# One transformer block on one core: AV sums in column groups and turned by DMA, tokens of a tile ordered by parity, more LN1 turned by DMA, a modulation loaded in pieces, up evicted to bf16 by ScalarE, and a new order

## The chip, the core and the metric

The kernel runs on one NeuronCore of a Trainium2 chip. The core has five engines that take their instructions in order and wait for each other by semaphores: TensorE (PE, matmuls; its weight loads are shown apart as PEld), VectorE (DVE), ScalarE (ACT), GpSimd (POOL) and SyncE (SP), which here only issues DMAs. The metric is the device time of the kernel in microseconds. Three runs of the kernel before took 248.26, 248.86 and 251.65 us; the median is 248.86.

## The reference

S = 2048 tokens, D = 512, 32 heads of 16, a feed-forward width F = 1792, all bf16. Cut to what matters:

```python
mod = (silu(c) @ w_mod).reshape(1, 6, 1, -1)
sa, ca, ga, sb, cb, gb = ...            # six vectors of 512
h = layernorm(x) * (1 + ca) + sa
x = x + ga * A(h, wqkv, wo)
h = layernorm(x) * (1 + cb) + sb
x = x + gb * B(h, w1, w3, w2)

def A(x, wqkv, wo):                     # sliding local attention, W = 8, dilation 2
    q, k, v = heads(x @ wqkv)
    idx = pos[:, None] - 2 * arange(8)  # each token sees itself and 7 tokens of its own parity before it
    logits = einsum('bhsd,bhswd->bhsw', q, k[idx]) * 16 ** -0.5, masked where idx < 0
    o = einsum('bhsw,bhswd->bhsd', softmax(logits), v[idx])
    return o.reshape(B, S, D) @ wo

def B(x, w1, w3, w2):
    return (silu(x @ w1) * (x @ w3)) @ w2
```

## The kernel before

**How a program is made.** `_build` records operations, each with an engine, a function that emits its instructions, a cost and the values that it reads and writes. `Program.place` then sets them in the order of a literal list, `ORDER`, and gives each pooled buffer the slot that the literal list `SLOTS` names; `synchronize` adds the semaphore waits that follow from data and from buffer reuse. Each engine gets its share of `ORDER` and runs it strictly in order, SP's DMA issues included. So an instruction that waits holds back everything behind it on its engine. Nearly all DMAs are issued on SP, in L124, and one on ACT.

**Tiles.** The tokens are 16 tiles of 128. LN1 works on the groups of `LN1`, two tiles twice and then four tiles three times. The feed-forward part works on the groups of `FFN`: two, two, four, four, two and two tiles. Attention works on the `BLOCKS`, pairs of tiles.

**Start.** 26 matmuls on a constant (`warm`, L472) run while x and weights load. `modulation(0)` (L457) multiplies silu(c) with the first 1024 columns of w_mod, 32 matmuls of one column each, and writes shift and scale of LN1 to `modc`. `modulation(1)` does the same for LN2; `gate` (L485, L495) makes the two gates, with which wo (L876) and w2 (L882) are scaled.

**LN1 and projections.** `ln_stats` takes mean and variance on DVE (L509, L510) and the power on POOL, and writes the normalized rows `xn` (L521). `ln_T` turns them, features on partitions: with PE transposes (L581), whose eviction on ACT applies scale and shift (L589), or, for groups numbered from `DMA_T` on, with a DMA transpose on SP followed by one ACT pass (L566). `DMA_T = (5, 2)`: none of LN1, and LN2 from its third group on. `proj_qk` (L634) makes q and k, features on partitions, evicted on ACT (L642, L643); `proj_v` (L653) makes v, tokens on partitions, evicted (L663) and stored to a scratch tensor in DRAM.

**Attention of a tile.** DVE multiplies q with the eight shifted k (L684, 4096 elements per partition). PE sums over a head with 16 matmuls of 256 columns (L694): the weights are a 0/1 matrix `E` of 32 columns, and each matmul writes one of four groups of 32 output partitions, one group for 32 consecutive tokens. The softmax works in PSUM (L706, L711 on DVE, exp L724 on ACT, L736 to L739 on DVE). Its result `attn` is turned by PE (L749) and evicted (L753), so that partitions hold 16 tokens x 8 window places. Four DMAs per tile gather the shifted v from the scratch tensor in that layout (`vsh`, four times 256 KB), DVE multiplies (L769), and PE sums over the window:

```python
for g in range(8):
    for ft in range(KT):
        ins = e.matmul(b[:, ft * P + 16 * g:ft * P + 16 * g + 16], vv.at[:, g, ft * P:(ft + 1) * P], ind[:],
                       start=True, stop=True)
```

Here (L778) vsh is the stationary side and the 0/1 matrix `ind` of 16 columns moves, so the output already has features on partitions. ACT evicts it (L788), reordering tokens, and PE multiplies with wo (L795); DVE adds the residual and keeps its row sum (L799).

**Feed-forward.** Each of the 14 units of a group is four matmuls with w1 and four with w3 (L811), a silu on ACT (L817), and a product on DVE that reads `up` from PSUM (L820). w2 (L849, and L837 for the last two tiles) sums the 14 units; DVE adds the residual (L859), and SP stores the output. FFN units of early groups stand among the attention of later tiles in `ORDER`.

Of the kernel before, what the change touches and what calls it, by code (L numbers as in the profile page):

```python
# [248 lines left out]
C_PQ, C_RED, C_ACC = 2203, 455, 800  # L249
# [17 lines left out]
NWARM = 18  # L267
DMA_T = (5, 2)
# [3 lines left out]
def _build(p, A_x, A_wqkv, A_wo, B_w1, B_w3, B_w2, c, w_mod, out):  # L272
# [4 lines left out]
    x_view = x2d.rearrange("(t p) d -> p t d", p=P)  # L277
# [18 lines left out]
    atb = [sb([P, 2, 32, W], bf, f"attn{i}") for i in range(NSM)]  # L296
# [3 lines left out]
    otb = [sb([P, KT, P], bf, f"ot{i}") for i in range(2)]  # L300
# [3 lines left out]
    E_sb = sb([P, KT, H], bf, "E")  # L304
    ones = sb([P, 512], bf, "ones")
    ind = sb([P, 16], bf, "ind")
    before = sb([P, W, 2, 16], bf, "before")
# [8 lines left out]
    csT_bf = sb([P, KT], bf, "csT_bf")  # L316
    gcol = sb([P, 8], bf, "gcol")
    modc = sb([P, 16], f32, "modc")

# [32 lines left out]
    otpool = Pool("ot", otb)  # L352
    hhpool = Pool("hh", [])
    tmppool = Pool("tmp", [])

    def held(pool, items):

        vals = []
        for i, item in enumerate(items):
# [12 lines left out]
                                           pattern=[[-1, P]], channel_multiplier=1), 300, k, w=[vident])  # L372
    p.op("pool", lambda e: e.memset(cst[:, 0:1], EPS), 80, k, part=[vcst])
# [3 lines left out]
    p.op("pool", lambda e: e.affine_select(out=E_sb[:], in_=E_sb[:], compare_op=ALU.is_ge, fill=0.0, base=0,  # L377
                                           pattern=[[128, KT], [-16, H]], channel_multiplier=1), 320, k, w=[vE])
    p.op("pool", lambda e: e.affine_select(out=E_sb[:], in_=E_sb[:], compare_op=ALU.is_ge, fill=0.0, base=15,
                                           pattern=[[-128, KT], [16, H]], channel_multiplier=-1), 320, k, w=[vE])  # L380
    p.op("pool", lambda e: e.memset(ind[:], 1.0), 100, k, w=[vind])
    p.op("pool", lambda e: e.affine_select(out=ind[:], in_=ind[:], compare_op=ALU.is_ge, fill=0.0, base=0,
                                           pattern=[[-W, 16]], channel_multiplier=1), 200, k, w=[vind])
    p.op("pool", lambda e: e.affine_select(out=ind[:], in_=ind[:], compare_op=ALU.is_ge, fill=0.0, base=W - 1,
                                           pattern=[[W, 16]], channel_multiplier=-1), 200, k, w=[vind])
    p.op("pool", lambda e: e.memset(before[:], 0.0), 250, k, w=[vbefore])
    p.op("pool", lambda e: e.affine_select(out=before[:], in_=before[:], compare_op=ALU.is_ge, fill=BEFORE, base=0,
                                           pattern=[[-DIL, W], [1, 2], [2, 16]], channel_multiplier=0), 400, k, w=[vbefore])
# [10 lines left out]
    p.dma(x_sb[:, 0:2, :], x_view[:, 0:2, :], ("load", 1), (256, 1024), w=vx[0:2])  # L399
    p.dma(wm_s[0][:], wm_view[:, :, 0:1024], ("load", 2), (512, 2048), w=[vwms[0]])  # L400
    p.dma(x_sb[:, 2:4, :], x_view[:, 2:4, :], ("load", 27), (256, 1024), w=vx[2:4])
# [4 lines left out]
    for g in range(1, 4):  # L406
        p.dma(x_sb[:, 4 * g:4 * g + 4, :], x_view[:, 4 * g:4 * g + 4, :], ("load", 5 + g), (512, 1024), w=vx[4 * g:4 * g + 4])
# [35 lines left out]
    p.op("dve", lambda e: e.tensor_copy(csT_bf[:], bank(vpc).bitcast(bf)[:, 0:KT]), 180, ("mod", 1), r=[vpc], w=[vcs])  # L443
# [4 lines left out]
    def modulation(i):  # L448
        k = ("mod", 2 + i)
        vm = Val("ps_mod", psum)  # L450
        jlo = 8 * i

        def mm(e):
            b = bank(vm)
            for j in range(8):
                for t in range(KT):
                    ins = e.matmul(b[:, j:j + 1], wm_s[i][:, t, j * P:(j + 1) * P], csT_bf[:, t:t + 1], start=(t == 0),  # L457
                                   stop=(t == KT - 1))
            return ins

        o = p.op("pe", mm, 32 * 26, k, r=[vwms[i], vcs] + wm_hold, w=[vm])
        p.op("dve", lambda e: e.tensor_copy(modc[:, jlo:jlo + 4], bank(vm)[:, 0:4]), 180, k, r=[vm], part=[vmod[i]])
        p.op("dve", lambda e: e.tensor_scalar(modc[:, jlo + 4:jlo + 8], bank(vm)[:, 4:8], 1.0, None, op0=ALU.add), 180, k,
             r=[vm], part=[vmod[i]])
        return o

    def warm(i, after=()):

        vw = Val("ps_warm", psum)

        def mm(e):
            return e.matmul(bank(vw), ones[:, 0:P], ones[:], start=True, stop=True)  # L472

        p.op("pe", mm, 428 if i < 10 else 232, ("warm", i), r=[vc], w=[vw], after=after)

    def gate(i):
# [4 lines left out]
        def mm(e):  # L481
            b = bank(vm)
            for j in range(4):
                for t in range(KT):
                    ins = e.matmul(b[:, j:j + 1], wm_g[i][:, t, j * P:(j + 1) * P], csT_bf[:, t:t + 1], start=(t == 0),  # L485
                                   stop=(t == KT - 1))
            return ins
# [132 lines left out]
    def proj_qk(gi, Ts, kind, vh):  # L620
# [6 lines left out]
        for ft in range(KT):  # L627
# [3 lines left out]
            def mm(e, ts, ft=ft, vp=vp):  # L631
                col = kind * D + ft * P
# [7 lines left out]
            def ev(e, ft=ft, vp=vp):  # L640
                if kind == 0:
                    return e.activation(dstv.at[:, ft, at0:at0 + n], bank(vp)[:, 0:n], ACT.Copy, scale=SCALE)  # L642
                return e.activation(kT[:, ft, PAD + 512 * cch + at0:PAD + 512 * cch + at0 + n], bank(vp)[:, 0:n], ACT.Copy)  # L643
# [3 lines left out]
    def proj_v(T, tt, vh):  # L647
# [19 lines left out]
        p.dma(v_dram[PAD + T * P:PAD + (T + 1) * P, :], lambda: vt.at[:], k, (128, 1024), r=[vt], w=[vd], cost=400, store=True)  # L667
# [5 lines left out]
    def logits(Ts):  # L673

        vl = Val("ps_l", psum)
        for i, T in enumerate(Ts):
# [10 lines left out]

            def red(e, i=i, T=T, vp=vp):
                c0 = vl.at * 512 + i * W * 32
                if T == 0:  # L690
                    e.matmul(PALL[0:32, c0:c0 + W * 32], ones[:, 0:32], before[:], start=True, stop=False, tile_position=(0, 0))
                for ft in range(KT):
                    for q in range(4):
                        ins = e.matmul(PALL[32 * q:32 * q + 32, c0:c0 + W * 32], E_sb[:, ft, :], bass.AP(vp.at, ft * P + 32 * q, [[W * KT * P, P], [KT * P, W], [1, 2], [2, 16]]),  # L694
                                       start=(ft == 0 and (T > 0 or q > 0)), stop=(ft == KT - 1), tile_position=(0, 32 * q))
# [35 lines left out]
    def softmax(Ts, vl, ve, vx_):  # L731
# [7 lines left out]
        p.op("dve", lambda e: e.tensor_tensor(ve.at[0][:, 0:n], bass.AP(PALL, bank(vl).offset, [[8 * 512, P], [W * 32, n], [1, 32], [32, W]]),  # L739
                                              bass.AP(ve.at[2], 0, [[64, P], [32, n], [1, 32], [0, W]]), ALU.mult),  # L740
             74 + 267 * n, k, r=[vr, vx_], w=[va], hold=[ve, vl], lead=o, lock=False)
        vt, val = Val("ps_at", psum), Val("al", alpool)

        def turn(e):
            b = bank(vt).bitcast(bf)
            for i in range(n):
                at = b[:, i * 256:(i + 1) * 256].rearrange("p (q y h) -> p q y h", q=4, y=2)
                for y in range(2):
                    ins = e.transpose(at[:, :, y, :], bass.AP(ve.at[0], i * W * 32 + y * 16 * W, [[2 * W * 32, P], [1, P]]), ident[:])  # L749
# [7 lines left out]
    def values(T, i, val):  # L757
# [3 lines left out]
        for q in range(4):  # L761
            p.dma(lambda q=q: vv.at[:, 2 * q:2 * q + 2, :],
                  bass.AP(v_dram, (PAD + T * P + 32 * q) * D, [[2 * D, 16], [-DIL * D, W], [1, 2 * D]]), ("vl", T), (128, 2048),
# [8 lines left out]
        vo = Val("ps_o", psum)  # L772

        def acc(e):
            b = bank(vo)
            for g in range(8):
                for ft in range(KT):
                    ins = e.matmul(b[:, ft * P + 16 * g:ft * P + 16 * g + 16], vv.at[:, g, ft * P:(ft + 1) * P], ind[:],  # L778
                                   start=True, stop=True)
            return ins  # L780

        p.op("pe", acc, C_ACC, ("ac", T), r=[vv, vind], w=[vo])
        vt = Val("ot", otpool)

        def ev(e):
            dst = bass.AP(vt.at, 0, [[KT * P, P], [32, 4 * KT], [1, 2], [2, 16]])
            src = bass.AP(PALL, bank(vo).offset, [[8 * 512, P], [32, 4 * KT], [16, 2], [1, 16]])
            return e.activation(dst, src, ACT.Copy)  # L788

        p.op("act", ev, c_act(512), ("ac", T), r=[vo], w=[vt])  # L790
# [13 lines left out]
    def ffn_unit(gi, n, fi, vh, after):  # L804
# [4 lines left out]
        def mm(e, vp, wt):  # L809
            for t in range(KT):  # L810
# [9 lines left out]
        p.op("dve", lambda e: e.tensor_tensor(vh_.at[:, 0:n], vt.at[:, 0:n], bank(vup)[:, 0:n], ALU.mult), c_dve(n), k,  # L820
             r=[vt, vup], w=[vh_])
# [35 lines left out]
    def store(T, c0, n, vz):  # L857
        vo = Val("o", opool)
        p.op("dve", lambda e: e.tensor_tensor(vo.at[:, 0:n], bank(vz)[:, 0:n], x_sb[:, T, c0:c0 + n], ALU.add),  # L859
             c_dve(n), ("zo", T), r=[vz, vx[T]], w=[vo])  # L860
        finals.append(p.dma(out2d[T * P:(T + 1) * P, c0:c0 + n], lambda: vo.at[:, 0:n], ("zo", T), (128, 2 * n), r=[vo], cost=400, store=True))

    for i in range(NWARM):
        warm(i)
    first = modulation(0)
    for i in range(8):
        warm(NWARM + i, [first])
# [12 lines left out]
    for g in range(NG):  # L880
        a, b = cuts[g], cuts[g + 1]
# [19 lines left out]
    p.late = list(late.values())  # L901
    p.gates = [d[T] for T in range(NT) for d in (prods, avs)]
    for o, n in zip(p.late, GATES):
        if n >= 0:
            o.deps[p.gates[n]] = True
# [98 lines left out]
```

## Time and profile before

| | |
|---|---|
| device time, median of three runs | 248.86 us (248.26 to 251.65) |
| span of the profiled execution | 248.5 us |
| PE / DVE / ACT / POOL busy | 239.7 / 180.1 / 138.3 / 23.9 us |
| DMA moved | 35.74 MB in 33711 packets, 52.0% of 16 engines' span on the SP queue |
| granted TensorE clock | 1.000 |
| AV sums, L778 | 512 matmuls, 0.78 to 0.96 us for the 32 of a tile |
| logit sums, L694 | 256 matmuls of 256 columns |
| products in the FFN, L820 | 84 on DVE, 39.3 us |

The profile is of one execution, whose span runs from the first to the last instruction; its time is not told apart from the span, which lies 0.36 us below the median of the runs. Matmuls are pipelined, so the mean duration of one matmul in a group is longer than the distance to the next; the chain of work in order of time gives the distance. The same holds, less, for DVE and ACT, where two instructions in a row overlap by some 0.1 us: one L663 eviction lasts 0.60 us, two in a row span 1.09. An issue's "landing" is the time from its issue on SP to its completion.

### The profile page before, as it was taken

To read this page: it belongs to the slowest core of one execution; us is meant where nothing else is said; L and a number is where in the kernel's file an instruction comes from. 1 tells how busy PE (TensorE), PEld (TensorE's weight loads), DVE (VectorE), ACT (ScalarE), POOL (GpSimd) and SP (SyncE) were. 2 spreads that over 40 slices of the span, in tenths; PEclk is the share of its full clock that TensorE was granted. 3 is DMA by queue.
4 is the path that set the end of the run, shared out by engine and by line. 5 is a ranking of instruction groups with operands and counts; after the bars stand their busy time and mean duration, and the time that the engine had idled before them with its cause. 6 is when DMAs were issued, how large, how long until landed. Compare 5 with 4: busy or idle time off the path is not lost.

```text
span 248.5 us, 5309 instructions
## 1 busy us (share of the span) xinstructions
PE 239.7 (96%) x2194; PEld 148.5 (60%) x2224; DVE 180.1 (72%) x273; ACT 138.3 (56%) x273; POOL 23.9 (10%) x66
## 2 busy tenths in 40 slices
PE   7999998799999999999999999999999999999995
PEld 2587454458964549776544464455455556687864
DVE  4488997799999999999988998873182432452542
ACT  2189684699455799447659775263557305442300
POOL 6130200010300200022031002000100100000000
PEclk9999999999999999999999999999999999999999
DMA  6989799999903607886354828916002002100001
GB/s 222 355 265 289 207 246 331 299 320 268 303 18 78 176 3 191 243 247 170 28 150 131 228 66 209 192 21 193 0 14 52 3 0 63 63 3 21 3 34 51
DMA packets 33711, 35.74 MB, mean 144 GB/s; under 512 B 8584, under 2 KB 24984, under 8 KB 33688
## 3 DMA queue, kind: packets, MB, share of 16 engines
q1 hardware_dynamic: 33680, 35.42, 52.0%
q8 instruction: 17, 0.28, 0.5%
q14 instruction: 6, 0.05, 0.1%
q10 hardware_dynamic: 8, 0.00, 0.0%
HBM read 29.62 MB, written 4.21 MB: 136 GB/s over the span
## 4 chain that ended last, share of the span: by engine, by line
PE 89%; DVE 3%; DMA 3%; issue 2%; SPq 1%; ACT 0%; DVEq 0%
PE pall L811 39%; PE pall L849 17%; PE pall L634 7%; PE pall L795 5%; PE pall L778 5%; PE pall L653 4%; PE pall L472 3%; PE pall L694 3%; DMA sb_vsh<-v_scratch_dram 3%; PE pall L837 2%; PE pall L581 2%; SPq L124 1%; DVE sb_pq L684 1%; PE pall L457 1%; PE pall L749 1%
## 5 line engine op out<-in xcount | busy, mean ns | idle before, releaser
L811 PE MATMUL pall<-sb_h,sb_w 128*128 128x256 bf16 (+1 forms) x664 | 102.4, 307 | 0.4
L811 PEld LDWEIGHTS pall<-sb_h,sb_w 128*128 128x128 bf16 x672 | 64.5, 98 | 33.0 <-issue 0.6
L820 DVE TENSOR_TENSOR sb_hh<-sb_sg,pall 128x256 bf16<-128x256 bf16 (+1 forms) x84 | 39.3, 503 | 32.3 <-PE pall L811 28.7
L817 ACT ACTIVATE sb_sg<-pall 128x256 bf16<-128x256 f32 (+1 forms) x84 | 35.2, 453 | 47.4 <-PE pall L811 39.7
L849 PE MATMUL pall<-sb_w,sb_hh 128*128 128x512 bf16 x187 | 43.6, 379 | 0.6 <-issue 0.2
L684 DVE TENSOR_TENSOR sb_pq<-sb_q,sb_kT 128x4096 bf16<-128x4096 bf16 x16 | 36.3, 2282 | 0.1
L634 PE MATMUL pall<-sb_h,sb_wqkv 128*128 128x512 bf16 (+1 forms) x154 | 31.1, 335 | 1.0 <-DMA sb_wm_s<-in_w_mod_dram 0.6
L849 PEld LDWEIGHTS pall<-sb_w,sb_hh 128*128 128x128 bf16 x196 | 18.9, 98 | 20.7 <-issue 0.2
L769 DVE TENSOR_TENSOR sb_vsh<-sb_vsh,sb_al 128x4096 bf16<-128x4096 bf16 x12 | 27.3, 2286 | 2.0 <-DMA sb_vsh<-v_scratch_dram 2.0
L788 ACT ACTIVATE sb_ot<-pall 128x512 bf16<-128x512 f32 x16 | 11.9, 745 | 19.6 <-PE pall L778 19.5
L634 PEld LDWEIGHTS pall<-sb_h,sb_wqkv 128*128 128x128 bf16 x160 | 14.8, 97 | 10.9 <-ACT sb_v L663 0.7
L859 DVE TENSOR_TENSOR sb_o<-pall,sb_x 128x512 bf16<-128x512 f32 (+1 forms) x18 | 11.3, 629 | 13.4 <-DMA out_dram<-sb_o 7.2
L589 ACT ACTIVATE sb_h<-pall,sb_modc 128x256 bf16<-128x256 bf16 (+1 forms) x26 | 15.3, 669 | 10.0 <-PE pall L581 9.9
L653 PE MATMUL pall<-sb_wqkv,sb_h 128*128 128x512 bf16 x62 | 16.0, 379 | 0.1
L531 POOL TENSOR_SCALAR sb_nm<-sb_sx 128x2 f32<-128x2 f32 x8 | 3.7, 466 | 124.0 <-DVE sb_x L799 124.0
L799 DVE SCALAR_TENSOR_TENSOR sb_x<-pall,sb_x 128x512 bf16<-128x512 f32 x16 | 10.6, 686 | 6.3 <-PE pall L795 6.3
L795 PE MATMUL pall<-sb_wo,sb_ot 128*128 128x512 bf16 x60 | 14.7, 379 | 0.2
L535 ACT ACTIVATE sb_xn<-sb_x,sb_nm 128x512 bf16<-128x512 bf16 x16 | 11.5, 720 | 5.0 <-POOL sb_nm L531 4.9
L546 ACT ACTIVATE sb_xn<-sb_x,sb_nb,sb_rs 128x512 bf16<-128x512 bf16 x16 | 12.4, 810 | 3.2 <-POOL sb_nb L544 3.2
L778 PEld LDWEIGHTS pall<-sb_ind,sb_vsh 128*128 128x128 bf16 x384 | 11.1, 96 | 3.5 <-ACT sb_ot L788 1.5
L778 PE MATMUL pall<-sb_ind,sb_vsh 128*128 128x16 bf16 x384 | 11.4, 169 | 1.2 <-DVE sb_vsh L769 1.1
L509 DVE BATCH_NORM_STATS2 sb_st<-sb_x 128x6 f32<-128x512 bf16 x16 | 10.8, 672 | 2.3 <-DMA sb_x<-in_A_x_dram 2.3
(79 smaller groups left out, 224.7 us busy)
## 6 DMA issues: line engine op xcount, KB each, us to landing
sb_vsh<-v_scratch_dram SPq DMA_DIRECT2D x48, 256.0 KB, 4.9
sb_vshx<-v_scratch_dram SPq DMA_DIRECT2D x16, 256.0 KB, 4.1
sb_w<-in_B_w_dram SPq DMA_DIRECT2D x6, 512.0 KB, 9.3
sb_w<-in_B_w_dram SPq DMA_DIRECT2D x6, 384.0 KB, 6.9
v_scratch_dram<-sb_v SPq DMA_DIRECT2D x16, 128.0 KB, 3.7
out_dram<-sb_o SPq DMA_DIRECT2D x14, 128.0 KB, 1.9
sb_wqkv<-in_A_wqkv_dram SPq DMA_DIRECT2D x3, 512.0 KB, 7.8
sb_x<-in_A_x_dram SPq DMA_DIRECT2D x3, 512.0 KB, 9.1
```

The costliest lines, as they stand in the source:

```text
L546: p.op("act", lambda e, vn=vn, T=T: e.activation(vn.at[:], x_sb[:, T, :], ACT.Identity, bias=nb[:, T, :], scale=rs[:, NT + T, :]), c_act(5 ...
L589: return e.activation(vh.at[:, ft, 0:n * P], b[:, j * 512:j * 512 + n * P], ACT.Identity, bias=modc[:, 8 * which + ft:8 * which + ft + 1], ...
L634: ins = e.matmul(bank(vp)[:, 0:n], wqkv[:, t, col:col + P], vh.at[:, t, 0:n], start=(t == ORDER[0]), stop=(t == ORDER[-1]))
L653: ins = e.matmul(bank(vp), vh.at[:, t, tt * P:(tt + 1) * P], wqkv[:, t, 2 * D:3 * D], start=(t == ORDER[0]), stop=(t == ORDER[-1]))
L684: return e.tensor_tensor(vp.at[:], in0, in1, ALU.mult)
L769: return e.tensor_tensor(v_w, v_w, a_w, ALU.mult)
L778: ins = e.matmul(b[:, ft * P + 16 * g:ft * P + 16 * g + 16], vv.at[:, g, ft * P:(ft + 1) * P], ind[:], start=True, stop=True)
L795: ins = e.matmul(bank(vy), vt.at[:, ft, :], wo[:, ft, :], start=(ft == 0), stop=(ft == KT - 1))
L811: ins = e.matmul(bank(vp)[:, 0:n], wt[:, t, fi * P:(fi + 1) * P], vh.at[:, t, 0:n], start=(t == 0), stop=(t == KT - 1))
L817: p.op("act", lambda e: e.activation(vt.at[:, 0:n], bank(vgp)[:, 0:n], ACT.Silu), c_act(n), k, r=[vgp], w=[vt], table="silu")
L820: p.op("dve", lambda e: e.tensor_tensor(vh_.at[:, 0:n], vt.at[:, 0:n], bank(vup)[:, 0:n], ALU.mult), c_dve(n), k, r=[vt, vup], w=[vh_])
L849: ins = e.matmul(bank(vz), vhh[fi].at[:, tt * P:(tt + 1) * P], w2[:, fi, :], start=(fi == 0), stop=(fi == NF - 1))
```

## The change

The knobs: `DMA_T = (3, 2)` has LN1's tiles 8 to 15 turned by eight DMA transposes on SP. `NWARM` and `NWARM2` are 14 and 3, in all 17 matmuls where 26 were. `AVCOL` (all tiles) picks the new AV sum, `UPACT` (groups 0 to 3 of `FFN`, 56 units) the new eviction of up; `GBLATE` is off, so w2 is scaled as before. `GATES`, all -1 before, had no effect and is gone.

**Parity.** The 128 tokens of a tile stand on partitions with the 64 even ones first. Loads of x, stores of v and of the output are written so: x of tiles 0 and 1 in a DMA each, x of the others in DMAs of 64 partitions each. q and k keep the natural order in their buffers: their evictions write every other element. The features of q and k are interleaved, so that one `E` of 32 columns serves all four feature tiles; the weights for that are read with a step of four elements.

**AV.** With 32 tokens of one parity and four window places on the partitions of each gathered piece, the sum takes eight matmuls of 512 columns with the 0/1 matrix as the stationary side, 32 columns, in four column groups. The result has tokens on partitions; ACT evicts it contiguously (`oa`), and a DMA transpose on SP turns it into `ot`, which wo reads. The number and size of the gathers are the same. The last softmax product is two instructions of half the size.

**Modulation 0.** Its 1 MB of weights comes in four DMAs, one for each 128 rows, and the matmuls run piece by piece; the moving side, a slice of `csz`, has eight columns that are zero but for one, so that all products add up in the same eight output columns. One matmul more sets the base (0 or 1), and one copy replaces two DVE instructions.

**Up.** In the 56 units ACT copies up from PSUM to bf16 in SBUF, and DVE multiplies two bf16 tiles in SBUF.

**Order.** `ORDER` and `SLOTS` are new throughout. SP has 172 entries of DMA where 140 were: eight more loads, and 24 more transposes. On SP, the first eight gathers of v now stand ahead of all FFN weights, and behind four of the LN1 transposes; the q third of wqkv is the eleventh DMA, after 2 MB of x and w_mod. On PE, the first FFN unit stands behind all but two entries of the q and k projections, all but two of v, the logit sums of eight tiles and the AV sums of four.

```diff
-NWARM = 18
-DMA_T = (5, 2)
+NWARM = 14
+NWARM2 = 3
+DMA_T = (3, 2)
+AVCOL = frozenset(range(16))
+UPACT = frozenset((g, f) for g in range(4) for f in range(NF))
+GBLATE = False
...
-    p.dma(x_sb[:, 0:2, :], x_view[:, 0:2, :], ("load", 1), (256, 1024), w=vx[0:2])
-    p.dma(wm_s[0][:], wm_view[:, :, 0:1024], ("load", 2), (512, 2048), w=[vwms[0]])
...
+    def split_rows(a, row):
+        return bass.AP(a.tensor, a.offset + row * D, [[D, 2], [2 * D, P // 2], [1, D]])
+    def x_rows(T, n, r):
+        return bass.AP(x2d.tensor, x2d.offset + (T * P + r) * D, [[2 * D, P // 2], [P * D, n], [1, D]])
+    for T in range(2):
+        p.dma(x_sb[:, T, :], split_rows(x2d, T * P), ("load", 1), (128, 1024), w=[vx[T]])
+    for t in range(KT):
+        p.dma(wm_s[0][:, t, :], wm_view[:, t, 0:1024], ("load", 2), (128, 2048), w=[vwm0[t]])
+    for r in range(2):
+        p.dma(x_sb[64 * r:64 * r + 64, 2:4, :], x_rows(2, 2, r), ("load", 27), (128, 1024), part=vx[2:4])
...
+            if ts[0] == 0:
+                e.matmul(b[:, 0:8], ident[:], mbase[:], start=True, stop=False)
+            for t in ts:
+                for j in range(8):
+                    ins = e.matmul(b[:, 0:8], wm_s[i][:, t, j * P:(j + 1) * P], csz[:, t, 7 - j:15 - j], start=False,
+                                   stop=(t == KT - 1 and j == 7))
...
-                    ins = e.matmul(bank(vp)[:, 0:n], wqkv[:, t, col:col + P], vh.at[:, t, 0:n], start=(t == ORDER[0]),
+                    w_qk = bass.AP(wqkv, t * 3 * D + kind * D + ft, [[KT * 3 * D, P], [KT, P]])
+                    ins = e.matmul(bank(vp)[:, 0:n], w_qk, vh.at[:, t, 0:n], start=(t == ORDER[0]),
...
+                src = bank(vp)[:, 0:n].rearrange("p (t r m) -> p t r m", r=2, m=P // 2)
+                return e.activation(dst.rearrange("p (t m r) -> p t r m", r=2, m=P // 2), src, ACT.Copy,
+                                    scale=SCALE if kind == 0 else 1.0)
...
-        p.op("dve", lambda e: e.tensor_tensor(ve.at[0][:, 0:n], ..., ALU.mult),
+        for y in range(2):
+            o = p.op("dve", lambda e, y=y: e.tensor_tensor(bass.AP(ve.at[0], 128 * y, [[2 * W * 32, P], [W * 32, n], [1, 4], [4, 32]]),
...
-                    ins = e.matmul(b[:, ft * P + 16 * g:ft * P + 16 * g + 16], vv.at[:, g, ft * P:(ft + 1) * P], ind[:],
-                                   start=True, stop=True)
...
+                for y in range(2):
+                    for q in range(4):
+                        ins = e.matmul(b[32 * q:32 * q + 32, :], ind[:], vv.at[:, 4 * (q % 2) + 2 * y + q // 2, :], start=(y == 0),
+                                       stop=(y == 1), tile_position=(0, 32 * q))
...
+            p.op("act", lambda e: e.activation(va.at[:], bank(vo), ACT.Copy), c_act(512), ("ac", T), r=[vo], w=[va])
+            p.dma(lambda: vt.at[:], lambda: va.at[:], ("ac", T), (128, 1024), r=[va], w=[vt], cost=1250, transpose=True)
...
-        p.op("dve", lambda e: e.tensor_tensor(vh_.at[:, 0:n], vt.at[:, 0:n], bank(vup)[:, 0:n], ALU.mult), c_dve(n), k,
-             r=[vt, vup], w=[vh_])
+        if (gi, fi) in UPACT:
+            p.op("act", lambda e: e.activation(vh_.at[:, 0:n], bank(vup)[:, 0:n], ACT.Copy), c_act(n), k, r=[vup], w=[vh_])
+            p.op("dve", lambda e: e.tensor_tensor(vh_.at[:, 0:n], vt.at[:, 0:n], vh_.at[:, 0:n], ALU.mult), 60 + n * 69 // 128, k,
+                 r=[vt], w=[vh_], lock=True)
...
-GATES = [-1, -1, ...]
-ORDER = [16, 15, 3, 8, 0, ...]
+ORDER = [...]
```

More of the change, by code (lines that the diff above doesn't have):

```diff
@@ L295, in _build @@
     NSM = 3
-    atb = [sb([P, 2, 32, W], bf, f"attn{i}") for i in range(NSM)]
+    atb = [sb([P, 2, W, 32], bf, f"attn{i}") for i in range(NSM)]
     alb = [sb([P, 2, 8, H], bf, f"al{i}") for i in range(3)]
@@ L299, in _build @@
     ssb = [sb([P, 2, 32], f32, f"ssum{i}") for i in range(NSM)]
[L300 removed]
+    otb = [sb([P, KT, P], bf, f"ot{i}") for i in range(3)]
+    oab = [sb([P, D], bf, f"oa{i}") for i in range(2)]
     ga_bc = sb([P, D], bf, "ga_bc")
@@ L406, in _build @@
     for g in range(1, 4):
-        p.dma(x_sb[:, 4 * g:4 * g + 4, :], x_view[:, 4 * g:4 * g + 4, :], ("load", 5 + g), (512, 1024), w=vx[4 * g:4 * g + 4])
+        for r in range(2):
+            p.dma(x_sb[64 * r:64 * r + 64, 4 * g:4 * g + 4, :], x_rows(4 * g, 4, r), ("load", 5 + g), (256, 1024), part=vx[4 * g:4 * g + 4])
     late = {}
@@ L858, in store @@
         vo = Val("o", opool)
[L859 to L866, printed above, removed]
+        if GBLATE:
+            p.op("dve", lambda e: e.tensor_tensor(vo.at[:, 0:n], bank(vz)[:, 0:n], gb_bc[:, c0:c0 + n], ALU.mult),
+                 c_dve(n), ("zo", T), r=[vz, vg[1]], w=[vo])
+            p.op("dve", lambda e: e.tensor_tensor(vo.at[:, 0:n], vo.at[:, 0:n], x_sb[:, T, c0:c0 + n], ALU.add),
+                 60 + n * 69 // 128, ("zo", T), r=[vx[T]], w=[vo], lock=True)
+        else:
+            p.op("dve", lambda e: e.tensor_tensor(vo.at[:, 0:n], bank(vz)[:, 0:n], x_sb[:, T, c0:c0 + n], ALU.add),
+                 c_dve(n), ("zo", T), r=[vz, vx[T]], w=[vo])
+        finals.append(p.dma(bass.AP(out2d.tensor, out2d.offset + T * P * D + c0, [[D, 2], [2 * D, P // 2], [1, n]]), lambda: vo.at[:, 0:n], ("zo", T), (128, 2 * n), r=[vo], cost=400, store=True))
+    warms = [warm(i) for i in range(NWARM)]
+    first = modulation(0, warms)
+    for i in range(NWARM2):
         warm(NWARM + i, [first])
```

133 lines of the change are left out of this document (70 added, 63 removed), and 126 rows, old and new, of tables (ORDER, SLOTS).

## The prediction

> **What bounds the kernel now.** I read the busy shares first, then the forty slices.
>
> ```profile
> PE 239.7 (96%) x2194; PEld 148.5 (60%) x2224; DVE 180.1 (72%) x273; ACT 138.3 (56%) x273; POOL 23.9 (10%) x66
> ...
> PE   7999998799999999999999999999999999999995
> ...
> DVE  4488997799999999999988998873182432452542
> ACT  2189684699455799447659775263557305442300
> ...
> DMA  6989799999903607886354828916002002100001
> ```
>
> PE is full from slice 2 to the last but one, except in slices 7 and 8 (44 to 56 us). DVE is as full from 50 to 130 us but idles after; ACT has room. So matmul time removed anywhere comes off the end, and a wait put in front of a matmul is added. The chain in order of time gives the price of one PE job (start, length, what):
>
> ```profile
> 32.34 6.93 DMA sb_vsh<-v_scratch_dram
> ...
> 42.73 2.20 DVE sb_pq L684
> ...
> 48.71 0.94 PE pall L457 x32
> ...
> 69.31 0.11 PE pall L581 x2
> ...
> 80.85 0.99 PE pall L694 x32
> ...
> 119.27 0.78 PE pall L778 x32
> 120.08 0.96 PE pall L778 x32
> ...
> 245.89 0.42 DVE sb_o L859
> ```
>
> One tile's AV sum (L778) costs PE 0.78 to 0.96 us, one tile's logit sum (16 matmuls of L694) 0.5, two transposes 0.11. The chain leaves PE once: a gather of v landing at 39.3 makes DVE late, and PE pays before L457. The stage windows show how much (us, then busy time and count of PE, PEld, DVE, ACT, POOL, clock, DMA share, GB/s):
>
> ```profile
> 40.00:50.00 10.00, 7.30 (x117) 4.12 (x117) 8.52 (x13) 6.06 (x14) 0.55 (x3) 1.00 1.10 316
> 60.00:70.00 10.00, 10.00 (x123) 8.98 (x125) 9.86 (x21) 4.82 (x14) 1.88 (x4) 1.00 0.89 261
> ```
>
> 2.7 us of PE are lost from 40 to 50, with the DMA engines saturated. Last, the DMA transposes that LN2 already uses (tile view of sb_xn) and loads (the page):
>
> ```profile
> L124 SPq DMA_TRANSPOSE sb_h<-sb_xn x12: 1196/1264/1797, 109.9 to 207.9; - x12
> ...
> DMA to landing us min/median/max: 2.3/3.1/5.6
> ```
>
> ```profile
> sb_w<-in_B_w_dram SPq DMA_DIRECT2D x6, 512.0 KB, 9.3
> ...
> sb_wo<-in_A_wo_dram SPq DMA_DIRECT2D x4, 128.0 KB, 4.6
> ```
>
> A transpose holds SP 1.26 us and lands 3.1 after issue; a load behind a backlog takes 9.3.
>
> **Part by part.** *AV sums.* 32 matmuls of 16 columns become 8 of 512 in four column groups: 4096 columns, as many as L694's 16 of 256. In one group those would take 16 x 0.109 = 1.74 us (L811 at 256: 20 in 2.18), and take 0.50 to 0.55, so the groups overlap. I take 0.53 against a mean of 0.81: 16 x 0.28 = -4.5. Ends: 16 x 0.46 = -7.4, and, if 512-column groups did not overlap, 8 x 0.216 = 1.73 each, +14.7; L694 is the near row, same groups and types.
>
> *LN1 transposes of tiles 8 to 15* leave PE: 32 x 0.055 = -1.8.
>
> *Start.* Eight warm matmuls go, but the first projection needs wq, which in the new SP order ends the first 2.5 MB, as the second third of the projection weights does now; by the DMA issues that one landed at 10.7, the next at 12.2. Now PE starts at 10.7 too, but until 12.2 it does only four projections of 0.216 between warm matmuls, so in effect it is dense from 11.4. So -0.7 (ends 0 and -1.5). The modulation has one matmul more, at 0.03, and is done before wq: nothing. The POOL constants (0.1 each) precede that too.
>
> The rows of x now come in loads of 64 partitions. The nearest row is wo, in loads of 32, landing in 4.6 like the gathers around it: no cost. [...]
>
> *The gap at 46 us.* The new SP order puts the first eight gathers ahead of every FFN weight, where now w1, w2 and x loads are mixed among them. The gap should shrink. But by the rows DVE has 36 us of work up to its second AV product and starts near 4 (first x), so it ends near 40.5; PE, dense from 10.7, has work until 40.5 as well. That is no reserve, so I take -1.5 of 2.7 (ends 0 and -2.7).
>
> *The output turned by DMA.* wo now waits for eviction (0.60), SP, and landing (3.1; 5.6 at worst, beside gathers): 3.7 to 6.2 us after the AV sum. What cover stands between them on PE can be counted in the new order: for tile 1 sixteen 512-column projections and a spread, 3.7, plus wo of tile 0, 0.9: 4.6. Tiles 0, 1, 5, 7, 8 and 13 have 4.5 to 5.2, the others 5.6 to 12. At 3.7 nothing is lost; at 6.2 the six would lose 1.0 to 1.7 each, some 7 in all, as tiles 0 and 1 lose theirs together. Behind a waiting wo stands all of PE; behind a waiting transpose on SP, gathers and weights. I take 1.5, nearer to the median: +1.5 (ends 0 and 7).
>
> *LN1's DMA transposes.* On SP eight issues of 1.26 wait for DVE's normalized rows; v stores and gathers stand behind, and on ACT, in order, the modulation and evictions. At 3.1 us DMA still has earlier loads to move meanwhile: nothing (up to 12, below).
>
> *up through ACT.* 56 evictions, 28 x 0.385 + 28 x 0.60 (rows of L642) = 27.6 us more on ACT. DVE's products fall from 0.68 and 0.41 to about 0.34 and 0.21, worked out from L684 (4096 bf16 elements in 2.28): -15. ACT comes to 166 of 240 us, and PE's other FFN units hide the longer chain; if not, each unit costs up to 0.5. *Halved softmax products* add 0.6 on DVE, inside that. *Token parity* makes q and k evictions write every other element; L788, which scatters so, takes 0.745 against 0.60, so at most 40 x 0.145 = 6 more on ACT, in its idle time. The same parity costs stores, gathers and outputs no packets.
>
> *Weights of q and k read with a stride of four.* No row shows such a read. Packed loads follow each other every 24 ns (L778: 0.78 over 32). From 1 to 4 times that, 98 ns, hides under a 256-column matmul (0.109). I take nothing, nearest to the packed row; above it the end is 0.216 per load, for 64 matmuls +6.9.
>
> *SP* gets 24 transposes and 8 loads, some 34 us, and waits for over 150 us now, so its time is there; what its waits hold up is priced above. *The rest of the new order* moves the same matmuls about. I cost it at nothing, since FFN units without a tie to attention can fill PE from about 57 us on, as they do now; uncovered, one bad place costs what the gap at 46 cost, 2.7, either way. The second mask matmul of tile 0 adds 0.2, within rounding.
>
> **Sum**: -4.5 -1.8 -0.7 -1.5 +1.5 = -7.0, against the profiled span of 248.5: 241.5. The runs' median of 248.9 lies 0.4 above that span, so 241.9.
>
> **Rivals.** *The AV transposes come late* (14%): the 5.6 landings were taken beside gathers, and here each stands beside some; against it, most tiles have 5.6 or more of cover. The loss is 7 in place of 1.5: 247.4.
>
> *LN1's transposes are caught behind the loads* (12%), the slower side: DMA is 84 to 110% busy to 70 us. If they land like a weight load, 9.3 in place of 3.1, ACT stands 6.2 longer before each of two modulations, with the evictions that free PSUM for PE behind: +12.4, 254.3. It decides from about 3 us of lateness, and against it speaks that fewer loads are outstanding when they are issued.
>
> *Strided weights are slow* (7%): 248.8, no change. *Column groups do not overlap at 512* (3%), so the change does not do what it says: 16 x (1.73 - 0.53) = +19, 261. *The x halves come late* (2%): a later wq delays all of PE by one step in the landing of the weight thirds, 10.7 to 12.2 = 1.5: 243.4. The wo row speaks against it.
>
> **How the numbers follow.** The forecast has 62%, its own range 238 to 244: the ends of AV, start and gap on one side, 2 us more waiting on the other. A measurement of this kernel tells about 2%, 243.9 to 253.8. Faster: nearly all of the forecast, 0.62 with slivers of others. Same: late AV, strided weights, half of the LN1 case's spread, 0.27. Slower: 0.11. For 8 in 10 the range is 237.5 to 249.5, leaving out 6% below and the 14% of LN1 and column cases above.
>
> **What would show it.** Right: AV sums of 8 matmuls at 0.45 to 0.55; first projection near 10.7; PE over 9.8 of every 10 us from 20 to 60; wo's weight loads idle under 2 us in all behind DMA; q weight loads hidden. Wrong: idle of ACT before L566's counterpart, or of PE before wo, of several us; 256-column projections over 0.12 apart.

## The result and the profile after

| | before | after |
|---|---|---|
| median of 5 runs, us | 248.86 | 290.37 |
| lowest to highest, us | 247.54 to 251.65 | 290.11 to 292.01 |
| span of the profiled execution, us | 248.5 | 290.2 |

The ratio is 1.168, with a 95% interval of 1.160 to 1.176: 41.5 us slower, where 7 us less were forecast. The page of the profile after, the lines that answer to those of before (busy shares, forty slices of 7.25 us each, granted clock, DMA):

```profile
PE 248.8 (86%) x1802; PEld 140.2 (48%) x1802; DVE 171.5 (59%) x279; ACT 161.2 (56%) x329; POOL 26.3 (9%) x69
...
PE   6169995877695599998997999999989999999982
...
DVE  1377697595847079998997973982623331242521
ACT  2033945945584488974774679775467474323200
...
PEclk9999999999789699999998999999999999999998
DMA  5998496796555997389998128917051001010011
```

PE is no longer full from slice 2 on: it idles in slices 0 to 2, and on and off from 6 to 13 (43 to 102 us). No engine takes PE's place as the bound: DVE and ACT have their holes there too. And DMA, full to 70 us before, is at 6, 7, 9, 6, 5, 5 and 5 tenths in slices 6 to 12: PE waits for transfers while many DMA engines have nothing to do. The chain that ended last says for which transfers (start, length, what):

```profile
5.29 11.85 DMA sb_wm_s<-in_w_mod_dram
...
21.94 9.63 PE pall L661 x60
...
38.35 4.33 DMA sb_h<-sb_xn
42.68 0.40 SPq L124
43.12 8.30 DMA v_scratch_dram<-sb_v
...
56.58 4.88 DMA v_scratch_dram<-sb_v
...
68.47 8.65 DMA v_scratch_dram<-sb_v
...
87.59 9.35 DMA v_scratch_dram<-sb_v
...
116.93 0.44 PE pall L808 x8
```

The first projection (L661) starts at 21.9 us, not near 10.7. Then four times the chain goes through a *store* of v of 4.9 to 9.4 us; before, the same stores landed 3.7 us after issue in the median, and no store of v stood in the chain. (Further on, the chain holds two transposes of AV sums, 10.9 us, and three stores of the output, 15.7 us; those stores are written in the same way.) Who waits for a store of v? The view of the line that evicts v from PSUM on ACT, in the kernel before (L663) and after (L691):

```profile
L663 ACT ACTIVATE sb_v<-pall x16: 573/598/629, 13.3 to 93.2; 128x512 bf16<-128x512 f32 x16
its engine sat idle before it (us, times) until:
...
  DMA v_scratch_dram<-sb_v: 1.9, 1
```

```profile
L691 ACT ACTIVATE sb_v<-pall x16: 575/598/668, 33.6 to 117.2; 128x512 bf16<-128x512 f32 x16
its engine sat idle before it (us, times) until:
  DMA v_scratch_dram<-sb_v: 18.1, 5
```

An eviction needs one of a few buffers for v, and a buffer comes free when its store has landed. ACT works in order, so for 18.1 us it stood before five evictions, with the evictions that free PSUM for PE behind; before, it was 1.9 us. By the same view PE itself waited 13.4 us in all for this line. What the stores did in that time is seen in windows inside two of them (us, then PE, PEld, DVE, ACT, POOL, clock, DMA share, GB/s):

```profile
86.00:88.00 2.00, 2.00 (x13) 0.99 (x11) 1.99 (x2) 2.00 (x5) 0.00 (x0) 1.00 0.14 48
90.60:91.80 1.20, 0.54 (x4) 0.23 (x4) 1.20 (x3) 0.00 (x0) 0.00 (x0) 1.00 0.14 49
```

A DMA share of 0.14 is 0.14 x 16 = 2.2 busy engines, and 48 GB/s is what they move. The packets of data in these windows are 1 KB each and take 46 ns, so one store alone, 128 packets on two engines, would take 128 x 46 ns / 2 = 2.9 us, as an estimate. That other DMAs' packets on these two engines queue behind the stores, and the stores behind them, is my reading; the median landing of the gathers did not rise (4.3 us, before 4.9). The outermost dimension of the store's new access pattern has 2 entries too (even rows, odd rows), where it had 128. The semaphores changed with it: a store of v raises its own 16 times before and 3 times after, the last two within 0.4 us of each other, at its end. That the dimension sets the number of engines is an inference so far; the runs below test it.

Last, the clock is lower in places: windows of 10 us; the first has PE waiting 3.7 us at a clock of 1.00, the second and the third (0.79 and 0.81) lie over stretches at half clock, 75.7 to 82.5 and 96.2 to 103.0 us. The clock row misses one stretch: up to 28 us the 256-column matmuls of the first projection last 417 ns, and 272 ns from then on.

```profile
60.00:70.00 10.00, 6.32 (x44) 2.66 (x36) 6.40 (x6) 7.32 (x12) 0.00 (x0) 1.00 1.13 195
70.00:80.00 10.00, 6.76 (x51) 2.80 (x51) 8.62 (x11) 4.16 (x10) 1.51 (x4) 0.79 0.47 150
90.00:100.00 10.00, 3.53 (x28) 1.60 (x17) 3.50 (x5) 2.24 (x5) 0.00 (x0) 0.81 0.89 162
```

### The profile page after: what moved, and what is told of

It is laid out like the page before. It is cut to its first block, busy times and chain, and to the rows that moved or that the text cites. A ratio compares the mean times of both kernels' runs of the same rounds, so it can differ in the third digit from the quotient of the medians.

```text
span 290.2 us, 4603 instructions
## 1 busy us (share of the span) xinstructions
PE 248.8 (86%) x1802; PEld 140.2 (48%) x1802; DVE 171.5 (59%) x279; ACT 161.2 (56%) x329; POOL 26.3 (9%) x69
## 4 chain that ended last, share of the span: by engine, by line
PE 45%; DMA 29%; ACT 11%; DVE 7%; SPq 3%; POOL 2%; issue 2%; DVEq 0%; ACTq 0%
PE pall L848 22%; DMA v_scratch_dram<-sb_v 11%; PE pall L891 10%; PE pall L661 6%; DMA out_dram<-sb_o 5%; DMA sb_h<-sb_xn 5%; DMA sb_wm_s<-in_w_mod_dram 4%; DMA sb_ot<-sb_oa 4%; SPq L124 3%; PE pall L832 3%; ACT sb_h L593 2%; ACT sb_sg L854 2%; PE pall L808 2%; DVE sb_pq L712 2%; ACT sb_kT L670 1%
## 5 line engine op out<-in xcount | busy, mean ns | idle before, releaser
L848 PE MATMUL pall<-sb_h,sb_w 128*128 128x256 bf16 (+1 forms) x672 | 106.8, 313 | 9.9 <-ACT sb_v L691 6.5
L661 PE MATMUL pall<-sb_h,sb_wqkv 128*128 128x512 bf16 (+1 forms) x160 | 37.7, 392 | 7.4 <-ACT sb_v L691 3.2
L858 ACT ACTIVATE sb_hh<-pall 128x256 bf16<-128x256 f32 (+1 forms) x56 | 26.0, 489 | 11.8 <-PE pall L848 11.5
L859 DVE TENSOR_TENSOR sb_hh<-sb_sg,sb_hh 128x256 bf16<-128x256 bf16 (+1 forms) x56 | 17.6, 350 | 21.5 <-ACT sb_hh L858 20.5
L661 PEld LDWEIGHTS pall<-sb_h,sb_wqkv 128*128 128x128 bf16 x160 | 18.4, 124 | 22.3 <-ACT sb_v L691 5.3
L907 DVE TENSOR_TENSOR sb_o<-pall,sb_x 128x512 bf16<-128x512 f32 (+1 forms) x18 | 11.2, 627 | 20.3 <-DMA out_dram<-sb_o 11.4
L593 ACT ACTIVATE sb_h<-sb_h,sb_modc 128x512 bf16<-128x512 bf16 (+1 forms) x24 | 16.5, 734 | 10.9 <-DMA sb_h<-sb_xn 10.9
L691 ACT ACTIVATE sb_v<-pall 128x512 bf16<-128x512 f32 x16 | 9.5, 604 | 19.5 <-DMA v_scratch_dram<-sb_v 18.1
L862 DVE TENSOR_TENSOR sb_hh<-sb_sg,pall 128x256 bf16<-128x256 bf16 x28 | 11.1, 417 | 14.8 <-PE pall L848 13.8
L616 ACT ACTIVATE sb_h<-pall,sb_modc 128x256 bf16<-128x256 bf16 (+1 forms) x18 | 10.2, 620 | 16.0 <-PE pall L608 16.0
L670 ACT ACTIVATE sb_q<-pall 128x512 bf16<-128x512 f32 (+1 forms) x20 | 12.0, 636 | 6.7 <-PE pall L661 6.7
## 6 DMA issues: line engine op xcount, KB each, us to landing
sb_wqkv<-in_A_wqkv_dram SPq DMA_DIRECT2D x3, 512.0 KB, 12.7
```

Source lines behind the costliest of these rows:

```text
L593: return e.activation(vh.at[:, ft, 0:n * P], vh.at[:, ft, 0:n * P], ACT.Identity, bias=modc[:, 8 * which + ft:8 * which + ft + 1], scale=m ...
L661: ins = e.matmul(bank(vp)[:, 0:n], w_qk, vh.at[:, t, 0:n], start=(t == ORDER[0]), stop=(t == ORDER[-1]))
L670: return e.activation(dst.rearrange("p (t m r) -> p t r m", r=2, m=P // 2), src, ACT.Copy, scale=SCALE if kind == 0 else 1.0)
L848: ins = e.matmul(bank(vp)[:, 0:n], wt[:, t, fi * P:(fi + 1) * P], vh.at[:, t, 0:n], start=(t == 0), stop=(t == KT - 1))
L858: p.op("act", lambda e: e.activation(vh_.at[:, 0:n], bank(vup)[:, 0:n], ACT.Copy), c_act(n), k, r=[vup], w=[vh_])
```

## The experiments

Three theories. **A**: DMAs with an outermost dimension of 2 run on two engines (16 stores of v, 18 of the output, the loads of x for tiles 0 and 1). **B**: the 24 added DMA transposes hold the DMA engines. **C**: the loads of x for tiles 2 to 15, in 64 partitions, are slow. Kernels were timed beside the kernel before, whose median was 249.9, 251.1, 249.6 and 250.3 in the four sets, so each is given as a median and as a ratio to that (95% interval in brackets).

### Two engines: put in, and taken away

**The store of v alone, in the kernel before.**

```
-  p.dma(v_dram[PAD + T * P:PAD + (T + 1) * P, :], ...
+  p.dma(bass.AP(v_dram, (PAD + T * P) * D, [[D, 2], [2 * D, P // 2], [1, D]]), ...
```

> The kernel before, with one edit: each store of v walks its rows in DRAM as two runs of 64 (even, then odd rows), as the changed kernel does; the rows of a tile therefore stand in another order in the scratch and the attention mixes other tokens. Theory A (a DMA whose outermost dimension has 2 entries runs on 2 of the 16 DMA engines): a store of 128 packets of 46 ns then takes 128 x 46 / 2 = 2.9 us at least, gathers spread over all 16 engines queue behind it on those two, and DVE and PE wait: 255 to 270 us, with stretches of 2 busy engines in the trace. [...]

Measured: 268.3, ratio 1.076 (1.068 to 1.085). 18 us from one access pattern, with no DMA transpose of LN1 or AV and no 64-partition load of x in the kernel, so nothing in it on which B or C could act. The same two readings are there, the idle time before the eviction of v and a window inside a store:

```profile
L663 ACT ACTIVATE sb_v<-pall x16: 573/597/611, 12.0 to 109.4; 128x512 bf16<-128x512 f32 x16
its engine sat idle before it (us, times) until:
  DMA v_scratch_dram<-sb_v: 10.3, 4
```

```profile
48.00:50.00 2.00, 2.00 (x39) 1.37 (x38) 2.00 (x2) 1.15 (x3) 0.00 (x0) 1.00 0.14 48
```

**Four and sixteen runs of rows**, the same edit with `[[D, 4], [4 * D, P // 4], [1, D]]` and `[[D, 16], [16 * D, P // 16], [1, D]]`.

> The kernel before, each store of v walking its rows as 4 runs of 32 (every fourth row), where the first run had 2 runs of 64; other tokens are mixed, as there. If the number of engines follows the outermost dimension (theory A): 4 engines, 128 x 46 / 4 = 1.5 us a store, stretches of about 4 busy engines, and a third to a half of the first run's loss of 18 us: 253 to 259. If the loss came from the scattered rows in DRAM instead: 265 to 270, as with 2 runs.

> As the run before, with 16 runs of 8 rows. Theory A: all 16 engines, nothing lost: 248 to 251. Scattered rows: 265 to 270.

Measured: 254.9, ratio 1.017 (1.008 to 1.026), and 251.5, 1.007 (1.003 to 1.011). The loss goes 7.6%, 1.7%, 0.7% as the outermost dimension goes 2, 4, 16, with ever more scattered rows. A store raises its semaphore 3, 5 and 16 times in the three kernels; the load of c, with an outermost dimension of 4, raises its own 5 times in the kernels before and after. That this means 2, 4 and 16 engines is a reading: busy engines were measured for 2 alone, 2.2 by the share of 0.14. The loss follows the dimension, not the scatter. It falls faster than in proportion; that a store of half the length is mostly hidden is a guess. With 16 runs ACT's idle time before the eviction of v is 2.1 us, near the 1.9 of before. That run lies 0.5 us above theory A's range; scatter itself costs at most what is left there, 0.7% (up to 1.1% by the interval).

**The changed kernel, its narrow DMAs made wide.** Each is issued as two DMAs of 64 partitions, one for the even rows and one for the odd, so that both sides have 64 outermost. First the stores of v, then also tiles 0 and 1 of x and the output.

```
+  def half_rows(a, row, c0=0, n=D):
+      return tuple(bass.AP(a.tensor, a.offset + (row + r) * D + c0, [[2 * D, P // 2], [1, n]]) for r in range(2))
-  p.dma(split_rows(v_dram, PAD + T * P), lambda: vt.at[:], ...
+  p.dma(half_rows(v_dram, PAD + T * P), lambda: halves(vt.at), ..., parts=2)
```

> The changed kernel, each of the 16 stores of v issued as two DMAs of 64 partitions (outermost dimension 64 on both sides), same result. Theory A: PE's idle between 40 and 100 us, 17.8 us of 60, nearly goes and so does part of the low clock behind it: 268 to 276. Theory B: the gaps stay, since the transposes stay: over 286. Theory C: over 286, as the loads of x stay.

> As the run before, and the loads of x for tiles 0 and 1 and the 18 output stores as two DMAs of 64 partitions too, same result. Theory A: the first projection moves from 21.9 us to about 15, as two loads of 128 packets no longer lie on two engines; the tail is shorter by 1 to 3: 260 to 268. Theory C: the first projection stays near 20, as x for tiles 2 to 15 still comes in 64 partitions: 2 to 4 below the run before. Theory B: no change from the changed kernel.

Measured: 267.9, ratio 1.075 (1.067 to 1.083), and 259.7, 1.041 (1.032 to 1.049). From 1.168 the stores of v give back 9.3 points (23 us) and the others 3.4 more (8 us). In the second run wq, whose landing the chain holds (`8.25 7.49 DMA sb_wqkv<-in_A_wqkv_dram`), comes at 15.7 in place of 21.8. Both land 0.1 to 0.3 us below the ranges of theory A. Theory B falls: the transposes are all still there.

### 64 partitions: taken away, and put in

**Plain rows.** All of x, v and the output move in natural order, 128 partitions at a time, as many DMAs as in the changed kernel.

```
-  p.dma(split_rows(v_dram, PAD + T * P), ...
+  p.dma(v_dram[PAD + T * P:PAD + (T + 1) * P, :], ...
-  p.dma(x_sb[64 * r:64 * r + 64, 4 * g:4 * g + 4, :], x_rows(4 * g, 4, r), ...
+  p.dma(x_sb[:, 4 * g + 2 * r:4 * g + 2 * r + 2, :], x_pair(4 * g + 2 * r), ...
```

> The changed kernel with x, v and the output moved in natural row order and 128 partitions at a time: the ordering of tokens by parity is left out of the DMAs (not of the evictions), so the attention mixes other tokens; the number of DMAs is the same. Theory C: against the run before, wq lands at 10.7 to 12 and the first projection starts there: another 4 to 10 less, 250 to 258. Theory A alone: like the run before. Theory B: still over 280.

Measured: 249.8, ratio 1.001 (0.997 to 1.005). The whole loss of 41.5 us is gone: it was in how three kinds of DMA walk their rows. Theory C's range is met but for 0.2 us, and wq lands at 12.3, 0.3 us later than it gave.

**64 partitions put back into plain rows**, natural order: in x of tiles 2 to 15 (`x_sb[64 * r:64 * r + 64, ...]`, source rows `64 * r` on), in the stores of v alone, and in all of x, v and the output.

> The run with plain rows (249.8), with one edit: x of tiles 2 to 15 comes in DMAs of 64 partitions (the lower and the upper half, natural rows) in place of 128, as many DMAs and bytes as before; the parity order stays left out. If loads of 64 partitions are slow (theory C): wq lands 2 to 5 us later, packets of 1 KB take 75 to 90 ns in place of 51, and the time is 254 to 259, near the run with wide stores (259.7). If that run's 10 us came from the halves of v and of the output instead: 249 to 251.

> The run with plain rows (249.8; the parity order stays left out), with one edit: each store of v as two DMAs of 64 partitions, lower and upper half, natural rows. The run with x in halves cost 3.8 of the 10 us between wide stores and plain rows; if the halves of v are the rest (64 partitions and a second issue on SP each, in the full stretch to 70 us): 253 to 256. If the rest came from the two loads of tiles 0 and 1, every other row in the scratch, or the output: 249 to 251.

> The run with plain rows, with all of x, v and the output moved in DMAs of 64 partitions, natural rows, as many DMAs as in the run with wide stores; the parity order stays left out. Only the order of the rows differs from that run (259.7, 1.041 of before). If 64 partitions and the second issues are all of its distance to plain rows: 258 to 261. If every other row costs by itself: 254 to 257, the sum of the two runs with halves of x (1.011) and of v (1.014).

Measured: 253.6, ratio 1.011 (1.006 to 1.017); 253.9, 1.014 (1.009 to 1.020); 259.0, 1.037 (1.031 to 1.042). The last is the run with wide stores (1.041) but for the order of the rows, so 64 partitions, with the second issues where a DMA was halved, are nearly all of the distance to plain rows (3.6 of 4.0 points); 1.0 and 1.3 points come from x of tiles 2 to 15 and from v. The other 1.3 belong to tiles 0 and 1 of x, to the output, or to all halves acting together; no run parts them. The first run lies 0.4 us below its forecast, the others in theirs. The two windows show it: plain rows, then x in halves, from 12 to 15 us, with the DMA engines equally busy in both.

```profile
12.00:15.00 3.00, 2.92 (x16) 1.93 (x15) 3.00 (x9) 1.85 (x5) 0.70 (x2) 0.52 1.10 356
```

```profile
12.00:15.00 3.00, 1.80 (x10) 0.98 (x10) 2.61 (x7) 2.04 (x5) 0.00 (x0) 0.50 1.13 242
```

356 against 242 GB/s at a DMA share of 1.1, for packets of the same 1 KB: a mean of 50 ns each in the first and 76 in the second. wq lands at 15.0, 2.7 us later, and the stretch at half clock grows from 3.4 to 10.2 us. The 242 is a mix with loads of 128 partitions, and no view shows why the packets of the halves take longer.

### What is left when the transfers are mended

**The start, and a modulation moved**, both on plain rows. The first edit issues wq ahead of two loads of x and repeats two warm matmuls; the second, on top of it, puts the first modulation of tiles 12 to 15 two places later on ACT. In the list of the order:

```
-  ... x of tiles 4 to 7 (30, 31), wq (27) ...
+  ... wq (27), x of tiles 4 to 7 (30, 31) ...
-  ... modulation (320), gate's eviction (355), q's eviction (223), modulation (323) ...
+  ... gate's eviction (355), q's eviction (223), modulations (320, 323) ...
```

> The run with plain rows (249.8; the parity order stays left out), with wq issued ahead of the loads of x for tiles 4 to 7 and two warm matmuls repeated (6 and 3 times). The forecast failed at the start by 1.8 us (first projection at 12.5, not 10.7) and by 3.4 us at half clock; if both go: 246.5 to 248. Rival: PE waits later instead (x or wv later): 249 to 251.

> As the run before, and on ACT the first modulation of tiles 12 to 15 (which waits for the LN1 transposes turned by DMA) stands two instructions later, so that the eviction of the gate and one of q go ahead of it. If those evictions, held up on ACT, are PE's gap at 31 to 34 us (1.8 us): 0.5 to 1.8 less than the run before. Rival: the wait goes to the next projection of those tiles: no change.

Measured: 248.9, ratio 0.995 (0.992 to 0.999), and 249.1, 0.996 (0.992 to 1.000). The half clock is gone (the granted clock is 1.000), but the first projection only moves from 12.5 to 12.1: with wq landed at 10.6, PE waits for the normalized rows of tiles 2 and 3. The first forecast (246.5 to 248) is missed. The second edit removes the wait it aimed at, 1.8 us of PE behind the gate's eviction, and the time does not move, as its rival said. PE's longest waits in the first of the two:

```profile
PE pall L666 <- ACT sb_ga_bc L533: 1.8, 1, 1.8
PE pall L503 <- DVE sb_ones L375: 1.5, 1, 1.5
PE pall L837 <- DMA sb_ot<-sb_oa: 1.2, 1, 1.2
PE pall L613 <- DVE sb_xn L553: 1.2, 2, 0.6
PE pall L784 <- DVE sb_attn L773: 0.8, 2, 0.5
PE pall L853 <- ACT sb_hh L863: 0.8, 1, 0.8
...
```

There are many short ones. With the first gone, those for `sb_ot` grow from 1.2 to 1.8 and one of 0.7 for wv appears.

**Without up through ACT**, on plain rows: `UPACT = frozenset()`, the product taking the copy's place in the order; 125 places of the order shifted with it, as DVE's product now holds the PSUM bank.

> The run with plain rows (249.8), with up read by DVE from PSUM again in the 56 FFN units where the changed kernel evicts it by ACT (the parity order stays left out): 27 us less on ACT, 15 more on DVE. If the way through ACT costs nothing, as forecast: the same or up to 4 us more (DVE is full from 50 to 130 us): 249 to 254. If ACT's evictions are what is left of the loss: 246 to 248.5.

Measured: 269.9, ratio 1.076 (1.069 to 1.083), far outside both expectations. PE's first line of waits:

```profile
PE pall L851 <- DVE sb_hh L865: 10.2, 9, 3.0
```

PE waits for the banks until DVE's product has read them, where ACT freed them early. How much of the 20 us is the route itself and how much the shifted order, this run does not separate.

**The same result as the reference, with plain loads.** x arrives in plain rows for LN1, q and k are evicted in natural order, and the output is stored in two DMAs of 64 partitions; each tile of x is loaded once more in the order by parity for the residual, behind its gathers (first run), with the start as above (second), or behind its AV transpose (third, with the modulation moved too).

```
+  p.dma(halves(x_sb[:, T, :]), half_rows(x2d, T * P), ("xr", T), (128, 1024), w=[vx[T]], parts=2)
```

> The changed kernel with x, v and the evictions of q and k in natural order, 128 partitions at a time; the order by parity that the residual needs is made later: each tile of x is loaded again, in two DMAs of 64 partitions (every other row), behind that tile's gathers, and the output is stored in two such DMAs. Same result, 2 MB more of loads, 16 more issues on SP. If loads of 64 partitions cost only where the first projections wait for them (theory C, with A): 248 to 252, like the run with plain rows (249.8). Rival: the extra loads slow the gathers in the full stretch up to 70 us, and PE waits again: 253 to 258.

> As the run with the reload, and two edits at the start: wq is issued ahead of the two loads of x for tiles 4 to 7, and two of the warm matmuls become 6 and 3, so that PE does not stand idle before the modulation. If the forecast failed at the start because wq landed at 12.3 and because the idle time brought 3.4 us at half clock: the first projection at about 11, no stretch at half clock, 2 to 3 us less, 246 to 249. Rival: tiles 4 to 7 come later by as much as wq comes earlier, and PE waits there: no change against the run with the reload.

> The same result as the reference: the run with the reload and the start (253.0), with the second load of each tile of x issued behind the AV transpose of that tile in place of ahead of it, and the modulation moved as in the run before. If the reload cost 5 us because its transfers stood ahead of the AV transposes (wo waited 3.0 at 50 us, and half clock followed): 248 to 250.5. Rival: the bytes cost, not their place: 252 to 254.

Measured: 255.2, ratio 1.016 (1.009 to 1.022); 253.0, 1.011 (1.006 to 1.015); 257.7, 1.032 (1.026 to 1.037). Against plain rows the first run costs some 1.5 points, which hold the second loads and the output in halves together. It and the second land where their rivals stood. The third, whose two edits no run parts, is beyond both: the later place did not help, and my reading of the place was wrong. In the first run PE waited 3.6 us for AV transposes before wo, in the third 4.8. No version with the reference's result beats the kernel before.

## Why the prediction was wrong

**The step that failed** is one sentence under *up through ACT*: "The same parity costs stores, gathers and outputs no packets." The count of packets was right (the store has its 128 before and after), but I counted packets and did not ask on how many engines they go. They went on 2 of the 16 (2.2 by the share of 0.14), so that ACT stood 18.1 us before the buffers of v, and PE behind it. The term stood at 0; it measured 9.3 points for v and 3.4 for tiles 0 and 1 of x and the output, some 31 us. No rival held it, so 290 lay outside every case. The pattern `[[D, 2], ...]` stood in the diff.

**The x halves** were a term of 0 with a rival at 2% and 1.5 us. The rival was right and mis-sized: wq 2.7 us later, 1.0 point in all for x, and the halves of v, which the wide version needs, cost another 1.3. My counter-row, wo in 32 partitions landing in 4.6 us, did not bear on it: the same four loads land in 9.7 us in the changed kernel and in 8.8 on plain rows, so a landing gives no rate for x in halves. For tiles 0 and 1 the prediction has no term: they are one load each with two runs of rows, so theory A and not C holds for them, and tile 1 lands at 12.7 us in the changed kernel, at 5.3 on plain rows.

**The other terms can be read on plain rows**, where the transfers are mended:

- *AV sums*, -4.5: right. Its groups are 7.1 + 2.5 us of PE time in all, where they were 11.4 + 3.8; in the chain of the run with the start one tile takes 0.43 to 0.55, and 0.49 where two stand in a row. So the column groups overlap at 512: eight in a row, at the 0.216 of a 512-column projection, would be 1.73.
- *LN1 transposes off PE*, -1.8: right in kind; the groups of transposes go from 7.7 us for 80 records to 4.7 for 48, and each is 219 ns long in both.
- *Strided weights*, 0: right. Mean durations of 512-column projections stay at 379 and 380 ns, of 256-column ones at 272 and 273 (the run with the start, at full clock throughout). Their weight loads last 113 ns in the median where they lasted 98, and stay hidden.
- *The start*, -0.7: wrong, +1.8. wq landed at 12.3 and not 10.7: from 2 to 10 us the engines moved 271 GB/s where they moved 341. Eleven loads now stand up to it where five stood, at 0.43 to 0.47 us of SP each; that SP did not issue the small ones fast enough is the likely reason, not a tested one. 3.4 us at half clock followed, at most 1.7 us of work; PE's longest wait ahead of that stretch is 1.7 us, and the stretch is gone (clock 1.00 from 10 to 20 us, where it was 0.83) with wq earlier and the warm matmuls repeated. Which of the two edits took it away, and what brought it, no run shows.
- *The gap*, -1.5: it moved and hardly shrank. From 30 to 60 us PE loses 2.9 us before, 2.3 on plain rows and 3.0 in the run with the start. On plain rows 1.75 of it lie from 30 to 40 us, behind the LN1 transposes: ACT stands 1.9 us before the modulation, with the gate's eviction behind it. (The prediction puts the two slices in which PE is not full at 44 to 56 us; they are 37 to 50. Its sum uses the window of 40 to 50.) So the rival with LN1 (ACT standing there) holds, at 1.8 us and not 12.
- *wo behind its transpose*, +1.5: about right, 0.5 to 1.8 us in three plain runs; 3.5 in the changed kernel, where the transposes of AV landed in 2.3/3.8/6.8 us.
- *up through ACT*, 0: not shown to be worth nothing. In this order it frees the banks: without it PE waits 10.2 us for them in one line alone.

**The sum**, then: with all transfers mended the ratio is 1.001, and 0.995 with the start mended too, where 0.972 was forecast. PE is busy 235.6 us there against 239.7 before, so the work that left PE is real. Its named waits are 8.6 us against 4.4, so the time came back as waits of 0.2 to 1.8 us for DVE's normalized rows, ACT's evictions and the transposes. How these waits hang together is not settled by the runs; only the one behind the gate's eviction was taken away alone, and it gave nothing.

## What to carry to other kernels

When an access pattern changes, read its outermost dimension before anything else: a DMA that splits 128 rows into 2 interleaved runs moved 48 GB/s here, and the engine that needed its buffer waited, with all that stood behind it. A DMA share of 0.14 in the middle of a busy stretch, with transfers in the chain, was the sign. A reordering that is wanted for one consumer is best kept out of DMAs in a full stretch: mended by halves it still cost 4.1%, and by loading x twice 1.1 to 3.2%.

## What was not expected of the hardware

- Narrow stores took longer with another in flight: 2.9 us of work, as estimated from the packets, took 4.9 us in the chain for the store that had no other beside it, and 8.3 to 9.4 us for the three that had.
- The page lists no time of landing for the narrow stores; their delay shows in the chain, and by the idle time of the one who waits for the buffer.
- A load of 64 partitions keeps the DMA engines as busy (1.13 against 1.10) while moving a third less (242 against 356 GB/s), so the DMA share alone does not show it; GB/s beside it does.
